# Squares of the channel products from an SBUF copy, and another bank for each later batch's last state outputs

## The chip, the core and the metric

One core of a Trainium2 chip runs the whole program. The metric is device microseconds (us) of one execution; smaller is better. The core has a matrix engine (PE, whose weight loads are listed as PEld), a vector engine (DVE), a scalar engine (ACT), a small general engine (POOL), and DMA queues, which are issued here from SP. Matrix products land in PSUM, of which this kernel uses eight banks; ACT and DVE read them out to SBUF.

## What is computed

Four batches of 768 time steps with 384 channels go through three layers, one after the other:

```python
# 1. a complex linear recurrence per head (8 heads of 48), real part kept
S_re, S_im = ar * S_re - ai * S_im + k v^T,  ar * S_im + ai * S_re
y[t] = q[t] @ S_re
# 2. two pairs of products with a Relu between them
u = x + (relu(x^T @ w_tok1) @ w_tok2)^T
z = u + relu(u @ w_ch1) @ w_ch2
# 3. mixing with the step before, and a squared Relu
xk = mu_k * z + (1 - mu_k) * z_prev ;  xr = mu_r * z + (1 - mu_r) * z_prev
out = sigmoid(xr @ w_r) * (relu(xk @ w_k) ** 2 @ w_v)
```

`w_k` is 384 x 1024 and `w_v` 1024 x 384. Everything is float32 outside; inside, a number is split in two float16 parts (high and low) and a product of two such numbers takes three matrix products: high by high, high by low, low by high.

## The kernel before, in words

**Two streams.** A generator `attention(b)` makes layer 1 of batch b, in six blocks J of 128 time steps; a generator `dense(b)` makes layers 2 and 3. While `dense(b)` is issued, pieces of `attention(b + 1)` are issued between its pieces by a schedule of due times. The order of the instructions on each engine is then fixed at compile time by a planner, which has priorities (the `tc.high_priority` blocks: evacuations 400, the recurrence's matrix products 100) and its own estimate of each duration. On the chip every engine runs its list in that order, and waits at the head of it.

**Layer 3's first product.** `two_layers` runs through 16 items a batch (two halves t of the time steps, eight column blocks f). For an item, `wk1` issues nine matrix products into a PSUM tile `ps` of 128 x 384; `wk1_out` (lines 907 to 911) turns it into the two float16 parts of the square, `part[:, 0]` and `part[:, 1]`; `wv2` multiplies these with `w_v` in nine more products, which come in the program two items later (`LAG`). `ps` comes from a pool of two banks (`ps_d`), which the gate (`wr`) and the earlier layers use too. `wk1_out` squares in place: ACT does Relu (L908) and Square (L909) from `ps` to `ps`, ACT copies it to `part[:, 0]` (L910), and DVE subtracts that from `ps` to make `part[:, 1]` (L911). The bank is held until L911 has ended.

**Layer 1's outputs.** Each block J has a state product (`s_u`, bank tag `u`) and its outputs (`s_h`, bank tag `y`, in two groups g of four heads). Either tag has one bank in batches 2 to 4. For a head, `s_h` issues three products with the carried state `T16` (seen in the trace as `y<-CH,Rc 96*128`) and three with the masked scores `M16` (`y<-CH,Rc 128*128`). `M16` comes from the scores `sp` by DVE (`m<-sp,tri`), then ACT (`Rc<-m`), then DVE (`Rc<-m,Rc`). `s_i` reads the outputs out: ACT `xh<-y`, then DVE `xl<-y`, after which the bank is free for the next block. `s_u` of the last block, J = 5, issues nothing. The recurrence's products all have line L482 in the trace, and its ACT and DVE work line L337.

At the start of the next batch's layer 1, `X` (the decay inputs) is loaded by DMA, squared on ACT (`X<-X`, `wide<-X`) and added on DVE (`X<-X,wide`).

The SBUF tiles with tags `h1h` and `h1l` hold layer 2's first result (`h1`, 128 x 2 x 384 float16 each); they lie idle once `w_tok2` has been applied.

Of the kernel before, what the change touches and what calls it, by code (L numbers as in the profile page):

```python
# [8 lines left out]
F32 = mybir.dt.float32  # L9
# [4 lines left out]
ACTF = mybir.ActivationFunctionType  # L14
# [3 lines left out]
B, H, S, D = 4, 8, 768, 48  # L18
C = H * D
NJ = S // 128  # L20
# [35 lines left out]
X_S, U_S, XK_S, XR_S, SQ_S = 6, 5, 5, 3, 14  # L56
T1_S, T2_S, C1_S, C2_S, WK_S, WV_S, WR_S = 6, 5, 6, 7, 6, 6, 3
# [43 lines left out]
def split_path(  # L101
# [10 lines left out]
    MUL, ADD, SUB, MAX, MIN = ALU.mult, ALU.add, ALU.subtract, ALU.max, ALU.min  # L112
# [9 lines left out]
    TT = nc.vector.tensor_tensor  # L122
# [3 lines left out]
    ACT = nc.scalar.activation  # L126

    const = ctx.enter_context(tc.tile_pool(name="const", bufs=1))
    one = ctx.enter_context(tc.tile_pool(name="one", bufs=1))
# [56 lines left out]
    def seen(x):  # L186

        j = one.tile([128, LOW_N], F16, tag="seen", name="seen")
        if len(x.shape) == 3:
            j = j.rearrange("p (a f) -> p a f", a=x.shape[1])  # L190
        ACT(j, x, ACTF.Square, accum_out=col("low"))
# [126 lines left out]
    def hd(x):  # L318
        return x.rearrange("p (h d) -> p h d", h=H)
# [5 lines left out]
    last_ev = []  # L325
    tables = [None, [], []]

    def attention(b):
# [3 lines left out]
        st, hl, at = {}, {}, [None]  # L332

        def chained(fn, last):

            def call(*a, **k):
                ins = fn(*a, **k)  # L337
                if b == 0 and at[0] is not None:
                    last[:] = behind([ins], last)
                return ins  # L340

            return call

        on_act, on_dve = [], []
        ACT = chained(nc.scalar.activation, on_act)
        TT, STT = (chained(f, on_dve) for f in (nc.vector.tensor_tensor, nc.vector.scalar_tensor_tensor))
# [57 lines left out]
        def bank(tag, J, shape):  # L404
            if b == 0 and J % 2:
                return ps_a.tile(shape, F32, tag={"u": "a0", "y": "a1"}[tag], name=tag)
            return ps_1.tile(shape, F32, tag=tag, name=tag)
# [73 lines left out]
        def MM(**k):  # L481
            last_mm[:] = [nc.tensor.matmul(**k)]  # L482
            behind(last_mm, ahead if b == 0 else passed)
# [184 lines left out]
        def s_h(J, g):  # L668
            d = st[J]
            if g == 0:  # L670
                d["y"] = bank("y", J, [128, H, D])
            y = d["y"]
            with tc.high_priority(offset=P_PE):
                for h in range(4 * g, 4 * g + 4):
                    if J > 0:
                        th, tl = hd(T16[0:96, J % 2]), hd(T16[0:96, 2 + J % 2])
                        for n_, (a_, b_) in enumerate((("h", th), ("h", tl), ("l", th))):
                            MM(out=y[:, h], lhsT=Tr[J % 2]["q" + a_][0:96, h], rhs=b_[:, h], start=n_ == 0, stop=False)
                    if b == 0:
                        MM(out=y[:, h], lhsT=d["m", g][:, h % 4], rhs=d["v32"][:, h], start=J == 0, stop=True)  # L680
                    for n_, (m_, v_) in enumerate(((0, "vh"), (0, "vl"), (1, "vh")) if b > 0 else ()):
                        MM(out=y[:, h], lhsT=M16[g][m_][:, h % 4], rhs=d[v_][:, h], start=J == 0 and n_ == 0, stop=n_ == 2)
            return 0.0
# [24 lines left out]
        cq, ck = late(s_c, "q"), late(s_c, "k")  # L708
        fns = {"a": s_a, "x": s_x, "l": s_l, "b": s_b, "w": s_w, "q": cq, "k": ck, "e": s_e, "i": s_i, "u": s_u, "v": s_v}
        fns.update({nm + str(g): late(fn, g) for nm, fn in (("f", s_f), ("g", s_g), ("h", s_h), ("m", s_m)) for g in range(2)})  # L710
        order = [(x[0], fns[x[:-1]], int(x[-1])) for x in (ORD0 if b == 0 else ORD1).split()]

# [38 lines left out]
    def dense(b):  # L751
# [9 lines left out]
        h1 = [one.tile([128, 2, C], F16, tag=f"h1{s}", name=f"h1{s}") for s in "hl"]  # L761
        for f in range(2):
            need(("t1", f))
            if b == 0:
                ps = h1_ps[f][:, 0:N]
            else:
                ps = ps_d.tile([128, N], F32, tag="d", name="ps")
# [11 lines left out]
        u = [[two.tile([128, 3, N], F16, tag=f"u{s}", name=f"u{s}") for s in "hl"] for t in range(2)]  # L779
        for t in range(2):  # L780
            need(("t2", t))
            for c in range(3):
                ps = ps_d.tile([128, N], F32, tag="d", name="ps")
# [12 lines left out]
        def two_layers(nf, first, second, evac1, evac2, at=None):  # L796

            items = [(t, f) for t in range(2) for f in range(nf)]
            parts, acc = {}, {}
            for n_ in range(len(items) + LAG):  # L800
                if n_ < len(items):
                    t, f = items[n_]
                    ps = ps_d.tile([128, N], F32, tag="d", name="ps")
                    first(t, f, ps)
                    part = gring.tile([128, 2, N], F16, tag="g", name="g")
                    with tc.high_priority(offset=P_EV):
                        evac1(ps, part)
                        if n_ == 0:
                            seen(part[:, 0, 0:LOW_N])
                    parts[t, f] = part  # L810
                    yield 9 * MM
                    if at and n_ in at:
                        yield from at[n_]()
                if n_ >= LAG:
                    t, f = items[n_ - LAG]
                    if f == 0:
                        acc[t] = [ps_a.tile([128, N], F32, tag=f"a{i}", name=f"a{i}") for i in range(3)]
                    part = parts.pop((t, f))
                    for i in range(3):
                        second(t, f, i, part, acc[t][i], f == 0, f == nf - 1)  # L820
                        if f == nf - 1:
                            evac2(t, i, acc[t][i])
                    yield 9 * MM
# [8 lines left out]
            for c in range(3):  # L832
                mm3(ps, [w[:, c, 128 * f:128 * f + 128] for w in wc1], [x[:, c] for x in u[t]], c == 0, c == 2)

        def ch1_out(ps, part):
            ACT(part[:, 0], ps, ACTF.Relu)  # L836
            last_ev[:] = [STT(part[:, 1], ps, 0.0, part[:, 0], op0=MAX, op1=SUB)]  # L837

# [58 lines left out]

        NF = FC // 128
        yield from two_layers(NF, ch1, ch2, ch1_out, ch2_out, {NF + 10: lambda: gate(0)})


# [2 lines left out]
            for c in range(3):  # L904
                mm3(ps, [w[:, c, 128 * f:128 * f + 128] for w in wk], [x[:, c] for x in xk[t]], c == 0, c == 2)

        def wk1_out(ps, part):
            ACT(ps, ps, ACTF.Relu)  # L908
            ACT(ps, ps, ACTF.Square, scale=2.0 ** (SQ_S // 2 - XK_S - WK_S))  # L909
            ACT(part[:, 0], ps, ACTF.Copy)  # L910
            last_ev[:] = [TT(part[:, 1], ps, part[:, 0], op=SUB)]  # L911

        def wv2(t, f, jj, part, ps, start, stop):
            need(("v", f))
# [2 lines left out]
        def wv2_out(t, jj, ps):  # L917
# [4 lines left out]
            nc.sync.dma_start(out=out[b, 128 * J:128 * J + 128, :], in_=o)  # L922

        yield from two_layers(FK // 128, wk1, wv2, wk1_out, wv2_out, {FK // 128 + LAG: lambda: gate(1)})

    def run(gen, got, want):
# [319 lines left out]
```

## Time and profile before

| | us |
|---|---|
| median of 3 runs | 816.45 (816.13 to 817.19) |
| the profiled execution | 818.82 |
| its span, first to last instruction | 817.0 |
| PE busy in it | 741.3 (91%) |
| DVE busy | 581.8 (71%) |
| ACT busy | 522.6 (64%) |
| mean granted TensorE clock | 0.974 of full speed |

The profiled execution is 1.8 us longer than its span, and 2.4 us longer than the median. Busy time is what an engine spent in instructions; matrix products are pipelined, so that a row of 128 x 384 products shows 326 to 331 ns each while one starts every 0.16 us. Idle time of an engine is put down to the instruction that it waited for.

### The profile page before, as it was taken

The page shows a single profiled execution, that of the slowest core. Times are in us where ns is not written, and L with a number is a line of the kernel's source. Part 1 is how long each engine was busy: PE and PEld are TensorE (multiplying, and loading weights), DVE is VectorE, ACT ScalarE, POOL GpSimd, SP SyncE. Part 2 cuts the span into 40 slices and gives each one's busy share as a digit, 9 for nine tenths or more (in the row PEclk, how much of TensorE's full clock was granted, in tenths as well). Part 3 has the DMA queues.
Part 4 walks back from the last instruction along what each step waited for, and adds up shares of the span by engine and source line. Part 5 has one row for each costly group of instructions (what it writes and reads, how often), then busy time and mean ns, then how long its engine had stood idle before and what let it go on. Part 6 is the DMA issues. An engine that isn't in the chain of part 4 may idle for free.

```text
span 817.0 us, 15178 instructions
## 1 busy us (share of the span) xinstructions
PE 741.3 (91%) x6107; PEld 471.4 (58%) x6107; DVE 581.8 (71%) x1016; ACT 522.6 (64%) x988; POOL 21.3 (3%) x53
## 2 busy tenths in 40 slices
PE   0968878999989889999998989999999999999996
PEld 0557845455555455555665656566666666666553
DVE  3998978999998738887768448777776454484822
ACT  7884559777588779674568778566576532142752
POOL 3000000001010000000000000000000000010000
PEclk9987989999999999999999989999999999999998
DMA  8249983444673851052336331141333342868200
GB/s 273 78 118 205 195 264 136 130 154 118 176 137 82 194 120 49 20 122 55 62 63 120 91 85 49 46 104 26 63 62 63 81 134 79 268 198 261 103 30 33
DMA packets 137949, 94.92 MB, mean 116 GB/s; under 512 B 104592, under 2 KB 120208, under 8 KB 137872
## 3 DMA queue, kind: packets, MB, share of 16 engines
q1 hardware_dynamic: 137872, 93.88, 45.2%
q8 instruction: 50, 0.82, 0.4%
q14 instruction: 27, 0.22, 0.1%
HBM read 63.97 MB, written 4.72 MB: 84 GB/s over the span
## 4 chain that ended last, share of the span: by engine, by line
PE 47%; DVE 21%; ACT 15%; DMA 12%; issue 3%; SPq 1%; DVEq 0%; ACTq 0%
PE ps L741 22%; PE a L741 14%; PE y L482 4%; DVE X L337 4%; ACT X L337 3%; DMA X<-by_time_a_re_dram 3%; PE u L482 3%; DMA wst<-in_moe_w_k_dram 2%; DVE Wc L337 2%; PE sp L482 2%; ACT tmp L875 2%; DMA Rc<-qh 1%; DVE g L837 1%; DMA wst<-in_moe_w_v_dram 1%; DVE ql L337 1%
## 5 line engine op out<-in xcount | busy, mean ns | idle before, releaser
L741 PEld LDWEIGHTS <-wc 128*128 128x128 f16 x1728 | 166.7, 98 | 116.9 <-issue 9.5
L741 PE MATMUL ps<-uh,wc 128*128 128x384 f16 x576 | 156.3, 326 | 2.1 <-DVE ul L793 1.2
L741 PE MATMUL a<-g,wc 128*128 128x384 f16 x864 | 157.9, 326 | 0.0
L741 PE MATMUL ps<-xkh,wk 128*128 128x384 f16 x384 | 106.4, 331 | 3.5 <-DVE g L911 3.3
L741 PE MATMUL a<-wv,g 128*128 128x384 f16 x576 | 106.9, 328 | 2.5 <-ACT g L910 2.5
L836 ACT ACTIVATE g<-ps 128x384 f16<-128x384 f32 x96 | 46.4, 484 | 78.0 <-PE ps L741 76.6
L741 PE MATMUL ps<-ul,wc 128*128 128x384 f16 x288 | 93.8, 326 | 0.0
L482 PEld LDWEIGHTS <-Rc 96*128 96x128 f16 (+1 forms) x1416 | 69.8, 100 | 34.4 <-issue 13.9
L837 DVE SCALAR_TENSOR_TENSOR g<-ps,g 128x384 f16<-128x384 f32 x96 | 52.9, 554 | 37.4 <-ACT g L836 37.2
L741 PEld LDWEIGHTS <-wk 128*128 128x128 f16 x576 | 55.6, 99 | 39.9 <-issue 6.4
L741 PEld LDWEIGHTS <-g 128*128 128x128 f16 x576 | 54.9, 98 | 37.4 <-ACT g L910 3.0
L741 PE MATMUL ps<-xkl,wk 128*128 128x384 f16 x192 | 63.5, 331 | 0.0
L911 DVE TENSOR_TENSOR g<-ps,g 128x384 f16<-128x384 f32 x64 | 35.3, 553 | 35.1 <-ACT g L910 34.9
L482 PE MATMUL y<-CH,Rc 96*128 96x48 f16 (+1 forms) x912 | 42.9, 186 | 9.7 <-DVE xl L337 5.2
L908 ACT ACTIVATE ps<-ps 128x384 f32<-128x384 f32 x64 | 30.4, 476 | 30.9 <-PE ps L741 29.5
L337 DVE TENSOR_TENSOR m<-sp,tri 128x512 f32<-128x512 f32 x48 | 32.6, 685 | 20.5 <-PE sp L482 19.7
L482 PE MATMUL sp<-Rc 96*128 96x128 f16 x504 | 39.2, 225 | 8.6 <-DVE m L337 3.3
L337 DVE TENSOR_TENSOR Wc<-cs,X 128x768 f32<-128x768 f32 x48 | 44.8, 951 | 0.2
L337 ACT ACTIVATE X<-X 128x1152 f32<-128x1152 f32 x32 | 37.1, 1159 | 11.5 <-DMA X<-by_time_a_re_dram 9.6
L337 ACT ACTIVATE X<-X,col_c 128x1152 f32<-128x1152 f32 x32 | 40.0, 1252 | 1.2 <-DVE X L337 0.4
L482 PE MATMUL u<-CH,kh 128*128 128x48 f16 x320 | 36.2, 188 | 3.4 <-ACT kh L337 3.4
L337 DVE TENSOR_TENSOR Rc<-m,Rc 128x512 f16<-128x512 f32 x36 | 24.8, 689 | 18.6 <-ACT Rc L337 18.6
(212 smaller groups left out, 1377.9 us busy)
## 6 DMA issues: line engine op xcount, KB each, us to landing
wst<-in_moe_w_ch_dram SPq DMA_DIRECT2D x24, 768.0 KB, 4.4
CH<-in_qk_dram SPq DMA_DIRECT2D x18, 384.0 KB, 3.2
wst<-in_moe_w_tok_dram SPq DMA_DIRECT2D x8, 768.0 KB, 5.0
wst<-in_moe_w_k_dram SPq DMA_DIRECT2D x8, 768.0 KB, 4.5
wst<-in_moe_w_v_dram SPq DMA_DIRECT2D x8, 768.0 KB, 4.6
X<-by_time_a_re_dram SPq DMA_DIRECT2D x8, 576.0 KB, 4.8
X<-by_time_a_im_dram SPq DMA_DIRECT2D x8, 576.0 KB, 6.9
CH<-by_time_v_dram SPq DMA_DIRECT2D x24, 192.0 KB, 2.7
```

The lines of the kernel that those rows point to most:

```text
L337: ins = fn(*a, **k)
L482: last_mm[:] = [nc.tensor.matmul(**k)]
L741: ins = [nc.tensor.matmul(out=ps, lhsT=lh[a_], rhs=rh[b_], start=start and n_ == 0, stop=stop and n_ == 2) for n_, (a_, b_) in enumerate(( ...
L836: ACT(part[:, 0], ps, ACTF.Relu)
L837: last_ev[:] = [STT(part[:, 1], ps, 0.0, part[:, 0], op0=MAX, op1=SUB)]
L875: ACT(w[:, 0:N], z[:, 0:N], ACTF.Copy, scale=o[:, c:c + 1])
L908: ACT(ps, ps, ACTF.Relu)
L911: last_ev[:] = [TT(part[:, 1], ps, part[:, 0], op=SUB)]
```

## The change

Two edits. In `wk1_out` the Relu now goes from PSUM to a float32 SBUF tile `r` (in the idle `h1h` and `h1l` places, by the parity of f), with the scale that the Square had. In batch 1 (b == 0) ACT squares `r` in place and copies it to `part[:, 0]`, as before but from SBUF. In batches 2 to 4 ACT squares `r` straight into `part[:, 0]`, and DVE makes the float32 square by multiplying `r` with itself in place. DVE's subtraction then reads `r`. So `ps` has one reader, the Relu. In `s_h` the outputs of the last block of batches 2 to 4 use the bank tagged `u` in place of `y`. The argument f is passed on to both evacuation functions.

```diff
         def s_h(J, g):
             d = st[J]
             if g == 0:
-                d["y"] = bank("y", J, [128, H, D])
+                d["y"] = bank("u" if b > 0 and J == NJ - 1 else "y", J, [128, H, D])
...
-                        evac1(ps, part)
+                        evac1(ps, part, f)
...
-        def ch1_out(ps, part):
+        def ch1_out(ps, part, f):
...
-        def wk1_out(ps, part):
-            ACT(ps, ps, ACTF.Relu)
-            ACT(ps, ps, ACTF.Square, scale=2.0 ** (SQ_S // 2 - XK_S - WK_S))
-            ACT(part[:, 0], ps, ACTF.Copy)
-            last_ev[:] = [TT(part[:, 1], ps, part[:, 0], op=SUB)]
+        def wk1_out(ps, part, f):
+            r = one.tile([128, C], F32, tag=f"h1{'hl'[f % 2]}", name="r")
+            ACT(r, ps, ACTF.Relu, scale=2.0 ** (SQ_S // 2 - XK_S - WK_S))
+            if b == 0:
+                ACT(r, r, ACTF.Square)
+                ACT(part[:, 0], r, ACTF.Copy)
+            else:
+                ACT(part[:, 0], r, ACTF.Square)
+                TT(r, r, r, op=MUL)
+            last_ev[:] = [TT(part[:, 1], r, part[:, 0], op=SUB)]
```

## Rows read from the trace of the kernel before

**Rows 1.** The page's busy us, share of the span and instructions of each engine.

```profile
PE 741.3 (91%) x6107; PEld 471.4 (58%) x6107; DVE 581.8 (71%) x1016; ACT 522.6 (64%) x988; POOL 21.3 (3%) x53
```

**Rows 2.** Waits of PE: who waited for whom; us in total, times, longest.

```profile
PE y L482 <- DVE xl L337: 5.2, 2, 2.8
...
PE ps L741 <- DVE g L911: 3.3, 4, 2.6
...
PE a L741 <- ACT g L910: 2.5, 2, 1.3
```

**Rows 3.** Groups by line: xcount | busy us, mean ns | idle before, releaser.

```profile
L911 DVE TENSOR_TENSOR g<-ps,g 128x384 f16<-128x384 f32 x64 | 35.3, 553 | 35.1 <-ACT g L910 34.9
...
L910 ACT ACTIVATE g<-ps 128x384 f16<-128x384 f32 x64 | 30.9, 483 | 0.9
L908 ACT ACTIVATE ps<-ps 128x384 f32<-128x384 f32 x64 | 30.4, 476 | 30.9 <-PE ps L741 29.5 <-DVE g L911 1.4
```

**Rows 4.** Groups by line, the forms nearest to what is added.

```profile
L337 ACT ACTIVATE X<-u 128x384 f32<-128x384 f32 x24 | 11.7, 487 | 3.5 <-PE u L439 1.6 <-PE u L482 1.6
...
L877 ACT ACTIVATE xkh<-tmp 128x384 f16<-128x384 f32 x24 | 12.4, 516 | 2.5 <-DVE tmp L876 2.5
...
L864 DVE TENSOR_TENSOR tmp<-tmp,ul 128x384 f32<-128x384 f32 x18 | 8.9, 552 | 0.0
```

**Rows 5.** The chain that ended last, 784 to 806 us: start, us, what.

```profile
797.02 1.46 PE ps L741 x9
```

**Rows 6.** Timeline, 440 to 450 us: start, us, engine, line, operation.

```profile
442.31 0.47 ACT L908 ACTIVATE ps<-ps 128x384 f32<-128x384 f32 x1
...
445.49 0.47 ACT L909 ACTIVATE ps<-ps 128x384 f32<-128x384 f32 x1
445.62 1.36 DVE L337 TENSOR_TENSOR X<-X,wide 128x1152 f32<-128x1152 f32 x1 [2.04 <-ACT wide L337]
...
447.35 0.56 DVE L911 TENSOR_TENSOR g<-ps,g 128x384 f16<-128x384 f32 x1 [0.37 <-ACT g L910]
...
447.96 0.32 PE L741 MATMUL ps<-xkh,wk 128*128 128x384 f16 x1 [2.56 <-DVE g L911]
```

**Rows 7.** Timeline, 474 to 495 us.

```profile
481.21 0.47 ACT L908 ACTIVATE ps<-ps 128x384 f32<-128x384 f32 x1
...
483.90 0.62 ACT L337 ACTIVATE Rc<-m 128x512 f16<-128x512 f32 x1
...
485.06 0.68 DVE L337 TENSOR_TENSOR Rc<-m,Rc 128x512 f16<-128x512 f32 x1
485.19 0.20 PE L482 MATMUL y<-CH,Rc 96*128 96x48 f16 x1 [2.77 <-DVE xl L337]
```

**Rows 8.** Timeline, 296 to 312 us.

```profile
296.98 0.47 ACT L908 ACTIVATE ps<-ps 128x384 f32<-128x384 f32 x1 [0.86 <-PE ps L741]
...
302.73 0.55 DVE L911 TENSOR_TENSOR g<-ps,g 128x384 f16<-128x384 f32 x1
...
306.54 0.61 ACT L337 ACTIVATE Rc<-m 128x512 f16<-128x512 f32 x1
...
306.93 0.28 PE L482 MATMUL y<-CH,Rc 96*128 96x48 f16 x3 [2.39 <-DVE xl L337]
```

**Rows 9.** Stretches: us, busy us of PE, PEld, DVE, ACT, POOL, granted clock, DMA.

```profile
421.00:450.00 29.00, 25.64 (x242) 16.39 (x241) 24.27 (x47) 23.35 (x46) 0.00 (x0) 1.00 0.53 106
600.00:630.00 30.00, 28.15 (x269) 18.01 (x268) 23.04 (x47) 24.43 (x54) 0.00 (x0) 1.00 0.40 67
307.00:311.00 4.00, 4.00 (x43) 2.68 (x43) 3.82 (x6) 2.74 (x6) 0.00 (x0) 0.58 0.00 0
...
484.00:492.00 8.00, 6.81 (x55) 4.47 (x55) 4.81 (x8) 6.87 (x12) 0.00 (x0) 0.57 0.01 2
```

**Rows 10.** Groups by line on DVE, 421 to 450 us; then 600 to 630 us.

```profile
L911 DVE TENSOR_TENSOR g<-ps,g 128x384 f16<-128x384 f32 x6 | 3.3, 552 | 0.4 <-ACT g L910 0.4
...
L911 DVE TENSOR_TENSOR g<-ps,g 128x384 f16<-128x384 f32 x9 | 4.9, 552 | 0.4 <-ACT g L910 0.4
```

## The prediction, made before the changed kernel ran

> **What bounds the kernel now.** I read four views: the page's busy shares, the waits of PE, the timeline around the longest of those waits, and stretches for clock and load. PE is busy for 91% of the span, DVE for 71% and ACT for 64% [rows 1]. Towards the end, with no recurrence left, PE runs nine products in 1.46 us, back to back, and nothing else matters [rows 5]. So PE's own work is the floor, and the change adds and removes no matrix product. What can change is the time in which PE stands still. Three waits of PE lead to what is edited: outputs waiting for `xl` to leave the bank `y` (5.2 us, two times), first products waiting for L911 to free a `ps` bank (3.3 us, four times), and second products waiting for L910 (2.5 us, two times) [rows 2]. Together they are 11.0 us. [...]
>
> **The `ps` bank.** Before, an item's bank is held through Relu, Square, Copy and the subtraction; after, through the Relu alone. The largest case stands at 448 us: the Relu ended at 442.78, but L909 was at 445.49 and L911 at 447.35, and PE stood still for 2.56 us until it had ended [rows 6]. With the change the bank is free at 442.8, before PE begins to wait, so this wait goes. Next late is the second product of the same item. Its high part is the new Square, in L909's place, done at about 446.0. Its low part needs two DVE operations of 0.55 us, which queue behind `X<-X,wide`, which ends at 446.98 [rows 6]: about 448.1, where it was 447.9. The second products come in the list after nine first ones (1.46 us [rows 5]), so 445.4 + 1.46 = 446.9 is the soonest that they are wanted, and up to 1.2 us can come back for those that read the low part. I let half of it come back, so 2.0 us for this wait, and count all of the other three (3.3 - 2.56 = 0.74): 2.7 us. Bounds: 0 (the list places other waiting work there) and 3.3.
>
> **The bank of the last outputs.** `T16` is made from the same bank `u`, so outputs that read `T16` never find `u` occupied: this adds no wait. It removes the wait for `xl`, but not for `M16`, which the other half of the outputs reads. At 485 us PE resumed at 485.19; ACT's `Rc<-m` ended at 484.52 and DVE's `Rc<-m,Rc` at 485.74 [rows 7]. At 307 us PE resumed at 306.93, and `Rc<-m` ended at 307.15 [rows 8]. So alone this edit moves only the `T16` products forward, about 0.3 us for each of two ends; I take 0.6 us. Together with the bank edit more follows. At 303 us the bank freed by L911 at 303.28 would be free from the Relu that ended at 297.45 [rows 8], and at 485 us the Relu at 481.21 frees one at 481.68, inside the 2.77 us in which PE stood still [rows 7]. Nine first products (1.46 us [rows 5]) then fit into either wait, 2.9 us. Sum 3.5 us; bounds 0 and 5.2 [rows 2].
>
> **The head of each layer 3.** In batches 2 to 4 the high part is made by two ACT operations instead of three, so about 0.48 us [rows 3] less for each of the two waits for L910: 1.0 us. Bounds 0 and 2.5 [rows 2].
>
> **The clock.** The two stretches lose 0.42 x 4 = 1.7 and 0.43 x 8 = 3.4 us [rows 9], 5.1 us in all. They begin with waits of 2.4 and 2.8 us; the wait of 2.56 us at 448 us lies in a stretch at 1.00 [rows 6, 9], so length alone does not decide. With shorter waits the lower level may stay away or not. I take a third, 1.7 us; bounds 0 and 5.1.
>
> **What ACT and DVE pay.** Nothing in the trace is a Square from SBUF of this size; the nearest rows are 516 ns for an ACT operation from SBUF to float16 and 487 ns from PSUM to float32 SBUF [rows 4]. Before, three ACT operations take 476 + 476 + 483 = 1435 ns [rows 3]. Batch 1: 487 + 516 + 516 = 1519, 84 ns more for each of 16 items, 1.3 us on ACT, hidden behind PE where ACT is not what PE waits for. I take 0.5; bounds 0 and 1.3. Batches 2 to 4: 487 + 516 = 1003 ns, 0.43 us less for each of 48 items, 20.7 us of ACT, which is no bottleneck; I count no more for it than is counted above. DVE gets 48 multiplications; the nearest row, two float32 operands from SBUF, takes 552 ns [rows 4], 26.5 us in all. The subtraction now reads SBUF, 552 against 553 ns [rows 3, 4]: no change. The cover is DVE's idle time. It is thin at two heads of layer 3: DVE is busy for 24.27 of 29 us and 23.04 of 30 us [rows 9], with six and nine items [rows 10]. They become 24.27 + 6 x 0.55 = 27.6 (95%) and 23.04 + 9 x 0.55 = 28.0 (93%). Queued behind each multiplication are `m`, `Rc`, `xl` and the shifted inputs of the next half, and PE waits for those. I take 1.5 us; bounds 0 (the work all falls into the 4.7 and 7.0 us of idle time) and 15 x 0.55 = 8.3 (each delays PE in full).
>
> [...]
>
> **Sum.** 2.7 + 3.5 + 1.0 + 1.7 = 8.9 us gained; 0.5 + 1.5 = 2.0 us paid: -6.9 us. The profiled execution took 818.82 us, so 811.9 for one like it. It lies 2.4 us above the median of the runs, 816.45; the same step from the median gives 809.6 us, which I predict.
>
> **Rivals.** *The gaps stay, only what is waited for changes.* An engine's order is fixed, so an early bank is used only if the next instruction of PE's list needs it. For this rival: both long waits end when ACT and DVE catch up, and `M16` comes 0.2 to 0.5 us after the bank [rows 7, 8]; `m`, `Rc` and the second products all hang on the same DVE queue. Against: the 2.56 us at 448 are a wait for nothing but the bank [rows 6]. What is left is 0.7 for the short waits and 0.6 for the `T16` products, less 0.5: 0.8 us, so 815.6 us, within the 0.2% (1.6 us) that a measurement of this kernel can tell from no change.
>
> *DVE becomes the bound at the heads of batches 2 and 3* (the slower side). The place is the first 25 to 30 us of layer 3, the price up to 8.3 us. In this case the waits for banks turn into waits for the low part, so that only 0.7 (short waits), 0.6 (`T16`) and 1.0 (heads) stay gained, less 0.5 on ACT: 1.8 us. It decides once more than three of the 15 multiplications delay PE in full (4 x 0.55 = 2.2). Half of them: 8.3 / 2 - 1.8 = 2.3 us more, 818.8; all 15: 8.3 - 1.8 = 6.5 us more, 823.0. For it: 95% and 93%, and a low part whose chain now crosses from ACT to DVE once and then needs two operations there. Against: the evacuations have the highest priority of the planner, which knows the added work, and 4.7 us were idle.
>
> [...]
>
> **How the numbers follow.** Forecast 0.50, full clock 0.15, gaps stay 0.15, DVE the bound 0.20. The forecast's own range, from its bounds, is 805 to 814. The range that should hold 8 in 10 reaches down to the full clock's 803 and up to 818.5, into the half-delayed case of DVE; left out is most of the DVE rival and little below. Faster by over 0.2%: 0.50 + 0.15 and a third of the gaps case, 0.70. Within 0.2%: the rest of that and a little of DVE's, 0.13. Slower: 0.17.
>
> **What would show it.** The page's wait "first products for DVE L911" must be gone, and none for a Relu in its place of more than a few tenths. PE's wait for `xl` must be gone, replaced by one for `Rc` of under 1.5 us. The granted clock after 307 and 485 us (a few us earlier in the new trace) shows the clock's term. ACT's busy time should fall by about 19 us and DVE's rise by about 26; DVE in the first 30 us of layer 3 of batches 2 and 3 must have idle time left. The prediction is wrong if PE's waits for the subtraction, `m` or `Rc` grow there by more than 5 us, or if the planner sets PE's list so that the freed bank is not used.

## The result, and the profile after

The changed kernel took 809.9 us (median of four runs, 805.76 to 811.41) beside 816.82 us for the kernel before on the same chip: a ratio of 0.9894, 95% interval 0.9866 to 0.9922. In a later set it was 0.9902 (0.9882 to 0.9923). So it is faster by about 1%: 8 to 9 us by the ratios, 6.9 us between the two medians, where 6.9 were forecast; the forecast time of 809.6 rests on a median 0.4 us lower. The profiled execution took 809.93 us, its span 808.1.

The page's busy row, and some rows of the waits of PE:

```profile
PE 741.2 (92%) x6107; PEld 472.2 (58%) x6107; DVE 603.7 (75%) x1064; ACT 506.2 (63%) x940; POOL 21.2 (3%) x53
```

```profile
PE u L482 <- ACT Rc L337: 3.6, 2, 2.4
PE sp L482 <- DVE m L337: 3.5, 5, 1.5
...
PE y L482 <- DVE Rc L337: 2.2, 4, 0.8
...
PE u L482 <- DVE Rc L337: 1.2, 1, 1.2
...
PE a L741 <- DVE g L916: 0.8, 3, 0.4
```

Two of the three waits of [rows 2] are gone: nobody waits for `xl` to leave a bank, and no first product waits for the subtraction (now L916) or for the Relu that frees its bank now (L909). The third, for the high part, became 0.8 us for the low part. But in the place of the wait for `xl`, products of the recurrence now wait 3.6 us for ACT's `Rc`, a row that was not among the long ones before.

The groups of the evacuation answer to [rows 3, 4]:

```profile
L916 DVE TENSOR_TENSOR g<-r,g 128x384 f16<-128x384 f32 x64 | 35.5, 554 | 4.6 <-ACT g L912 3.2
...
L909 ACT ACTIVATE r<-ps 128x384 f32<-128x384 f32 x64 | 30.9, 482 | 33.5 <-PE ps L741 33.4
...
L915 DVE TENSOR_TENSOR r<-r 128x384 f32<-128x384 f32 x48 | 26.6, 553 | 24.3 <-ACT g L914 24.1
L914 ACT ACTIVATE g<-r 128x384 f16<-128x384 f32 x48 | 25.0, 521 | 1.1
```

DVE had the added 26.6 us of L915 and yet its busy time rose only from 581.8 to 603.7, by 21.9; ACT's fell by 16.4 us. Records of instructions that stand back to back overlap here (L915 at 446.06 us takes 0.56, and the next on DVE begins at 446.54, 0.08 before that ends; 48 x 0.08 is 3.8 us, as an estimate), so that busy time moved by less than the durations, and by less than the 26 and 19 us of the forecast.

**A stretch that starts at one instruction.** The spans contain a start-up that varies: the first product of layer 3 of batch 1 began between 227.3 and 232.5 us in the profiles of this study, where its work is the same. So I compare from that product to the end of the span. Columns as in [rows 9]; first the kernel before (all of it, then layer 3 of batch 2), then the kernel after:

```profile
232.44:817.00 584.56, 552.39 (x4557) 347.91 (x4554) 380.61 (x700) 358.48 (x711) 10.51 (x31) 0.98 0.38 96
...
422.06:496.02 73.96, 67.78 (x660) 44.43 (x658) 46.32 (x82) 59.08 (x103) 0.00 (x0) 0.95 0.40 88
```

```profile
231.93:808.10 576.17, 548.67 (x4557) 345.01 (x4554) 402.73 (x748) 342.00 (x663) 10.48 (x31) 0.99 0.39 97
...
420.27:488.93 68.66, 64.97 (x658) 42.33 (x656) 53.21 (x98) 53.53 (x87) 0.00 (x0) 1.00 0.42 94
```

The stretch is 8.4 us shorter, with the same 4557 products. PE's busy time fell by 552.39 - 548.67 = 3.7 us, and the rest, in which PE stood still, from 32.2 to 27.5, by 4.7. As an estimate from the granted clock, most of the 3.7 is the clock's (3.4, worked out in the part on the prediction). Layer 3 of batch 2 alone gives 5.3 us of the 8.4 (2.8 busy, 2.5 still), and its mean clock went from 0.95 to 1.00.

**Three places.** First the wait at 448 us of [rows 6]. The timeline of after, around the same products:

```profile
439.08 0.48 ACT L909 ACTIVATE r<-ps 128x384 f32<-128x384 f32 x1
...
443.53 0.33 PE L741 MATMUL ps<-xkh,wk 128*128 128x384 f16 x1
...
446.19 0.34 PE L741 MATMUL a<-wv,g 128*128 128x384 f16 x1 [0.25 <-DVE g L916]
```

The Relu, ended at 439.56, frees the bank 4.0 us before the first product at 443.53, and of the 2.56 us a wait of 0.25 for the low part is left.

Second, the end of batch 3's recurrence ([rows 7], then 485 us):

```profile
479.44 0.20 PE L482 MATMUL u<-CH,Rc 128*128 128x48 f16 x1 [1.17 <-ACT Rc L337]
...
481.49 0.65 PE L482 MATMUL u<-CH,Rc 128*128 128x48 f16 x19 [1.22 <-DVE Rc L337]
```

One wait of 2.77 became two of 1.17 and 1.22, for `Rc`.

Third, the end of batch 2's recurrence ([rows 8], then 307 us). Here nothing was won. First the kernel before, then after:

```profile
301.46 1.17 ACT L337 ACTIVATE X<-X 128x1152 f32<-128x1152 f32 x1 [2.98 <-DMA X<-by_time_a_re_dram]
301.46 1.35 DVE L384 TENSOR_REDUCE stat_rmin<-X 128x1 f32<-128x1152 f32 x1 [4.62 <-DMA X<-by_time_a_re_dram]
...
303.93 0.61 PE L482 MATMUL sp<-Rc 96*128 96x128 f16 x8 [1.31 <-DVE m L337]
```

```profile
298.68 1.17 ACT L337 ACTIVATE X<-X 128x1152 f32<-128x1152 f32 x1 [3.07 <-DMA X<-by_time_a_re_dram]
298.68 1.35 DVE L384 TENSOR_REDUCE stat_rmin<-X 128x1 f32<-128x1152 f32 x1 [4.81 <-DMA X<-by_time_a_re_dram]
...
300.12 1.28 ACT L337 ACT_TABLE_LOAD   x1 [0.27 <-DVE stat_rmin L384]
300.42 0.68 DVE L337 TENSOR_TENSOR m<-sp,tri 128x512 f32<-128x512 f32 x1
301.16 0.22 PE L482 MATMUL sp<-Rc 96*128 96x128 f16 x1 [1.51 <-DVE m L337]
...
303.73 0.63 ACT L337 ACTIVATE Rc<-m 128x512 f16<-128x512 f32 x1
...
304.41 0.26 PE L482 MATMUL u<-CH,Rc 128*128 128x48 f16 x2 [2.40 <-ACT Rc L337]
```

Read it from the top: ACT and DVE both stand at the decay inputs of the next batch, which have not landed (3.07 and 4.81 us; 2.98 and 4.62 before). `m` waits in DVE's queue behind them: after's products for it had ended by 297.91 us, and it began at 300.42, behind the minimum that stood at the load (298.68) and L916 (299.95). `Rc` waits in ACT's, behind the same load and then a table load (`ACT_TABLE_LOAD`, 1.28 us), more work on `X` and three shorter operations: `m` had ended at 301.10, and `Rc` began at 303.73. PE's list has recurrence products next. A free `ps` bank is of no use there: the next first product, at 304.57, stands in the list behind the ones that wait.

The stretches at the heads of batches 2 and 3, and at the ends of the recurrences:

```profile
419.00:448.00 29.00, 27.85 (x268) 17.90 (x267) 27.25 (x55) 22.04 (x43) 0.00 (x0) 1.00 0.54 107
593.00:623.00 30.00, 29.00 (x274) 18.50 (x272) 27.20 (x57) 21.14 (x45) 0.00 (x0) 1.00 0.41 67
302.00:310.00 8.00, 5.60 (x44) 3.29 (x44) 4.86 (x7) 6.47 (x12) 0.00 (x0) 0.57 0.03 6
...
476.00:484.00 8.00, 5.61 (x65) 3.69 (x63) 5.13 (x9) 7.97 (x12) 0.00 (x0) 1.00 0.01 2
```

DVE is at 27.25 of 29 and 27.20 of 30 us, with idle time left, as worked out (27.6 and 28.0). The clock was 1.00 in the 8 us from 476 and 0.57 in the 8 us from 302. In the other profiled execution of the same kernel (after, again) it was 0.79 over the same 8 us:

```profile
302.00:310.00 8.00, 6.30 (x68) 4.04 (x69) 5.18 (x8) 7.10 (x13) 0.00 (x0) 0.79 0.10 25
```

A third change lies in a place that the prediction did not look at. Before, PE waited 2.30 us in batch 1, and the clock behind it was 0.66 over 5 us; after, the wait is 0.48 and the clock 1.00. The wait and the stretch before, then both after:

```profile
278.90 0.65 PE L482 MATMUL y<-CH,Rc 128*128 128x48 f16 x19 [2.30 <-DVE Rc L337]
...
279.00:284.00 5.00, 5.00 (x38) 2.75 (x38) 4.64 (x6) 3.48 (x5) 0.00 (x0) 0.66 0.61 161
```

```profile
277.27 0.65 PE L482 MATMUL y<-CH,Rc 128*128 128x48 f16 x19 [0.48 <-DVE Rc L337]
...
279.00:284.00 5.00, 4.57 (x50) 2.86 (x48) 3.06 (x5) 4.71 (x9) 0.00 (x0) 1.00 0.11 40
```

### The profile page after: what moved, and what is told of

It reads as the page before. It is cut to its first block, busy times and chain, and to the rows that moved or that the text cites. A ratio compares the mean times of both kernels' runs of the same rounds, so it can differ in the third digit from the quotient of the medians.

```text
span 808.1 us, 15175 instructions
## 1 busy us (share of the span) xinstructions
PE 741.2 (92%) x6107; PEld 472.2 (58%) x6107; DVE 603.7 (75%) x1064; ACT 506.2 (63%) x940; POOL 21.2 (3%) x53
## 4 chain that ended last, share of the span: by engine, by line
PE 49%; DVE 24%; ACT 12%; DMA 11%; issue 3%; SPq 0%; DVEq 0%; ACTq 0%
PE ps L741 22%; PE a L741 16%; DVE X L337 4%; PE y L482 4%; ACT X L337 4%; PE u L482 3%; DVE Wc L337 2%; DMA X<-by_time_a_re_dram 2%; DMA wst<-in_moe_w_k_dram 2%; PE sp L482 2%; DVE tmp L876 2%; DVE g L837 1%; DMA wst<-in_moe_w_v_dram 1%; ACT L337 1%; DVE tmp L858 1%
## 5 line engine op out<-in xcount | busy, mean ns | idle before, releaser
L482 PEld LDWEIGHTS <-Rc 96*128 96x128 f16 (+1 forms) x1416 | 68.7, 100 | 36.0 <-issue 9.2
L909 ACT ACTIVATE r<-ps 128x384 f32<-128x384 f32 x64 | 30.9, 482 | 33.5 <-PE ps L741 33.4
L482 PE MATMUL sp<-Rc 96*128 96x128 f16 x504 | 38.3, 223 | 9.0 <-DVE m L337 3.5
L337 DVE TENSOR_TENSOR Wc<-cs,X 128x768 f32<-128x768 f32 x48 | 44.9, 953 | 0.1
L915 DVE TENSOR_TENSOR r<-r 128x384 f32<-128x384 f32 x48 | 26.6, 553 | 24.3 <-ACT g L914 24.1
L337 DVE TENSOR_TENSOR m<-sp,tri 128x512 f32<-128x512 f32 x48 | 32.6, 686 | 14.7 <-PE sp L482 14.5
L337 ACT ACTIVATE X<-X 128x1152 f32<-128x1152 f32 x32 | 37.0, 1160 | 10.3 <-DMA X<-by_time_a_re_dram 8.8
L337 ACT ACTIVATE X<-X,col_c 128x1152 f32<-128x1152 f32 x32 | 39.9, 1253 | 1.1 <-DVE Rc L337 0.4
L482 PE MATMUL u<-CH,kh 128*128 128x48 f16 x320 | 36.5, 188 | 3.5 <-ACT kh L337 3.4
L482 PE MATMUL y<-CH,Rc 96*128 96x48 f16 (+1 forms) x768 | 35.4, 184 | 4.1 <-DVE Rc L337 2.2
L916 DVE TENSOR_TENSOR g<-r,g 128x384 f16<-128x384 f32 x64 | 35.5, 554 | 4.6 <-ACT g L912 3.2
```

The costliest lines, as they stand in the source:

```text
L909: ACT(r, ps, ACTF.Relu, scale=2.0 ** (SQ_S // 2 - XK_S - WK_S))
L915: TT(r, r, r, op=MUL)
L916: last_ev[:] = [TT(part[:, 1], r, part[:, 0], op=SUB)]
```

## The experiments

Each kernel was timed in five rounds beside the kernel before; ratios are to that one, with 95% intervals. The last column is the stretch from layer 3's first product to the end in the profile (before 584.56, after 576.17). The first four kernels ran on one chip, the next four on a second and the last three on a third.

| kernel | median us | ratio | stretch us |
|---|---|---|---|
| only the outputs' bank | 816.93 | 0.9992 (0.9969 to 1.0014) | 586.56 |
| without the outputs' bank | 810.22 | 0.9913 (0.9885 to 0.9940) | 577.98 |
| after, `ps` held as long as before | 815.95 | 0.9978 (0.9951 to 1.0006) | 584.54 |
| three ACT operations in all batches | 809.49 | 0.9917 (0.9892 to 0.9943) | 578.71 |
| DVE multiplies in all batches | 804.54 | 0.9824 (0.9794 to 0.9853) | 572.29 |
| one more DVE operation, first halves | 813.94 | 0.9946 (0.9918 to 0.9973) | 581.33 |
| one more DVE operation, second halves | 810.25 | 0.9877 (0.9851 to 0.9903) | 576.90 |
| decay inputs behind the read-out | 804.61 | 0.9820 (0.9795 to 0.9844) | 571.74 |
| both that and DVE in all batches | 805.20 | 0.9849 (0.9826 to 0.9872) | 571.70 |
| the same, both halves behind | 807.78 | 0.9880 (0.9855 to 0.9904) | 575.06 |
| after, again | 809.43 | 0.9902 (0.9882 to 0.9923) | 575.81 |

Two limits hold for all that follows. An interval is about 2 us to either side, and that of a difference between two rows about 3; a stretch is that of one execution (after's two gave 576.17 and 575.81). And each kernel is planned anew, so that the lists of the engines differ in places from after's; no run holds the order fixed.

My theory was that the early release of `ps` carries most of the gain. The rivals were the outputs' bank, and ACT's shorter chain.

**Only the outputs' bank**: the kernel before with the edit in `s_h` alone.

```diff
-                d["y"] = bank("y", J, [128, H, D])
+                d["y"] = bank("u" if b > 0 and J == NJ - 1 else "y", J, [128, H, D])
```

> Only the outputs' bank is changed; the squares are made in PSUM as before. Bank theory (the gain of 7 us is the early release of the first products' bank): the outputs still wait for M16, so about 0.6 us less than before, 816.2 (815.3 to 816.8). Rival (the waits for xl and the low clock behind them, 5.2 + 5.1 us, are what the change removed): 807 to 811.

No change within the interval, which reaches from 2.5 us faster to 1.1 slower. Its middle, 0.7 us, is near the 0.6 of the prediction, but does not confirm it: the profile's stretch is 2.0 us longer than before's. Its waits of PE:

```profile
PE u L482 <- ACT Rc L337: 4.1, 2, 2.5
PE ps L741 <- DVE g L911: 3.9, 4, 3.1
```

The wait for `xl` has gone and one for `Rc` has come; the `ps` wait stays, its longest 3.1 us where it was 2.6.

**Without the outputs' bank**: the kernel after with that line put back.

> Only the squares are changed; the last outputs keep bank y. Bank theory: nearly the whole gain, 810 to 811.5, with no wait for L911 left in the trace and the wait for xl back at 485 us. Rival (outputs' bank): 813 to 816.5.

```profile
PE y L482 <- DVE xl L337: 4.9, 2, 2.6
```

The wait for `xl` is back with 4.9 us, and the time does not tell from that of after (0.9913 beside 0.9894 and 0.9902). So the other edit brings the gain. A wait of 5 us at the top of the list was worth 0.9 to 1.6 us by the middles of the ratios and about 2 by the stretch, which is not told from nothing: what follows it was late anyway.

**`ps` held as long as before**: a small copy reads the bank when the subtraction has been made, so that it comes free then; all else as in after.

```diff
             last_ev[:] = [TT(part[:, 1], r, part[:, 0], op=SUB)]
+            hold = one.tile([128, 1], F32, tag="cnt", name="hold")
+            behind([nc.vector.tensor_copy(hold, ps[:, 0:1])], last_ev)
```

> The changed kernel, with one DVE copy of a single column of ps added behind each subtraction, so that the bank is held as long as before although ACT has its two operations. It adds 64 DVE instructions of about 0.1 us. Bank theory: the waits for the bank come back, 2.7 + 2.9 us and part of the clock: 814.5 to 818. Rival (the 20 us that ACT is relieved of make the gain): within 1.5 us of the changed kernel, 810 to 811.5.

Most of the gain is gone: 0.9978. Its waits of PE, the longest of them for `m`, the copy's group, and the stretch:

```profile
PE sp L482 <- DVE m L337: 6.7, 6, 2.5
...
PE ps L741 <- DVE hold L918: 2.1, 4, 0.8
PE a L741 <- ACT g L914: 1.9, 2, 1.4
```

```profile
449.17 0.83 PE L482 MATMUL sp<-Rc 96*128 96x128 f16 x12 [2.48 <-DVE m L337]
```

```profile
L918 DVE COPY hold<-ps 128x1 f32<-128x1 f32 x64 | 9.6, 151 | 0.0
```

```profile
231.16:815.70 584.54, 552.25 (x4557) 345.99 (x4554) 407.85 (x812) 341.62 (x663) 10.51 (x31) 0.99 0.38 96
```

The copies themselves, 0.151 us each where about 0.1 was expected, cost something too. By the next experiment but one, DVE time in the first halves of batches 2 and 3 costs under half of itself: 16 copies there, some 1.1 us as an estimate; batch 1's eight at most 1.2. Of the (0.9978 - 0.9902) x 818 = 6.2 us that were lost, some 3.9 are thus the bank's by the middles of the intervals; no run has the copies without the hold. Busy time too is back at 552.25, 3.6 above after's. The granted clock shows a part of that: 0.98 from 419 to 495 us here and 1.00 from 420 to 489 in after, 0.02 x 76 = 1.5 us as an estimate. The wait for the bank itself came back only in part, 2.1 us with a longest of 0.8: at the place of the 2.56 us, PE now stands 2.48 us for `m`, because its list has products of the recurrence there.

**Three ACT operations in all batches**: ACT squares and copies as in batch 1, and DVE multiplies nowhere.

```diff
-            if b == 0:
-                ACT(r, r, ACTF.Square)
-                ACT(part[:, 0], r, ACTF.Copy)
-            else:
-                ACT(part[:, 0], r, ACTF.Square)
-                TT(r, r, r, op=MUL)
+            ACT(r, r, ACTF.Square)
+            ACT(part[:, 0], r, ACTF.Copy)
```

> The changed kernel with batch 1's form in all batches: three ACT operations, Square and Copy from SBUF, no multiplication on DVE. The bank is freed early, ACT is not relieved (0.08 us more than before for each item). Bank theory: 809 to 811.5, heads 1 us worse, DVE 1.5 us better. Rival (ACT's relief): 814 to 817.

Equal within the interval. So the gain needs neither ACT's relief nor DVE's multiplication: with the Relu moved out of PSUM, three ACT operations bring most of it too. Whether relief and load in batches 2 to 4 are both small or cancel (the prediction had 1.0 gained at the heads and 1.5 paid) is not told apart; the profile alone shows this kernel 2.5 us longer than after.

**One more DVE operation**, `TT(r, r, r, op=MAX)`, which changes no value, on the 16 items of the first halves of batches 2 and 3 (the heads), and in another kernel on the 16 of the second halves.

```diff
...
                 TT(r, r, r, op=MUL)
+                if b < 3 and t == 0:
+                    TT(r, r, r, op=MAX)
```

> The changed kernel with one more DVE operation of the same size (the larger of r and r, which changes nothing) for each of the 16 items in the first halves of layer 3 of batches 2 and 3, 8.8 us of DVE in the crowded stretches. Prediction's term (1.5 of 8.3 us reach PE): 811 to 813. Rival (DVE is the bound there already): 815 to 819. Free: 809 to 810.5.

> The same additional operation in the second halves (16 items, 8.8 us) of batches 2 and 3, where DVE is busy for half of the time. Both theories of the DVE term: no change, 809 to 811. If it is the longer chain of each item and not DVE's load that costs, as much as in the first halves.

In the heads 8.8 us of DVE cost (0.9946 - 0.9902) x 818 = 3.6 us, or 4.3 by after's first ratio; in the second halves nothing. Nearly all of the cost lies in batch 2: from its first product of layer 3 to batch 3's it took 177.9 us beside after's 173.7, and from there to batch 4's 154.5 beside 154.1, although DVE was fuller in batch 3. The windows of the heads in the first of the two:

```profile
418.00:447.00 29.00, 26.69 (x253) 16.68 (x252) 26.69 (x57) 19.35 (x37) 0.00 (x0) 1.00 0.42 92
596.00:626.00 30.00, 28.79 (x269) 18.20 (x266) 29.96 (x63) 21.32 (x45) 0.00 (x0) 1.00 0.34 67
```

Even with DVE at 29.96 of 30 us PE does 28.79 us of work: a full DVE did not by itself stop PE there. Why batch 2 pays and batch 3 does not was not tested.

**DVE multiplies in all batches**: batch 1 too takes two ACT operations and the multiplication.

```diff
-            if b == 0:
-                ACT(r, r, ACTF.Square)
-                ACT(part[:, 0], r, ACTF.Copy)
-            else:
-                ACT(part[:, 0], r, ACTF.Square)
-                TT(r, r, r, op=MUL)
+            ACT(part[:, 0], r, ACTF.Square)
+            TT(r, r, r, op=MUL)
```

> The changed kernel with the multiplication on DVE in batch 1 too (16 more, 8.8 us of DVE; ACT 16 operations fewer). DVE was busy for 28.5 of the first 30 us of batch 1's layer 3 before the change. If DVE work delays PE where DVE is full (the prediction's DVE term): 2 to 6 us slower than the changed kernel, 812 to 816. If DVE work is free even there: 809 to 811. If ACT is what matters in batch 1: 806 to 809.

It is faster than after by some 5 us (6.4 by the ratios, 3.9 by the stretches). The head of batch 1's layer 3:

```profile
227.00:257.00 30.00, 27.68 (x251) 16.82 (x250) 30.00 (x60) 24.11 (x52) 2.48 (x4) 1.00 0.44 84
```

In after, the first 30 us there show DVE at 29.19 and ACT at 27.49. So DVE was made full and ACT shorter by 3.4 us, and the time fell: DVE's load is not what PE hangs on in batch 1. The waits at 301 and 304 us of after are 0.80 and 1.65 us here, though ACT stands at the same load:

```profile
292.81 1.16 ACT L337 ACTIVATE X<-X 128x1152 f32<-128x1152 f32 x1 [3.39 <-DMA X<-by_time_a_re_dram]
...
296.25 0.62 ACT L337 ACTIVATE Rc<-m 128x512 f16<-128x512 f32 x1
...
298.98 1.28 ACT L337 ACT_TABLE_LOAD   x1
```

`Rc` stands ahead of the table load here, and behind it in after (303.73 and 300.12). This points to ACT's list; whether its length counts or its order, no run tells.

**Decay inputs behind the read-out.** This goes at the third place above: the squares and the minimum of the second half of the decay inputs of batches 3 and 4 are ordered behind the read-out (`xh`, `xl`) of the previous batch's last outputs, so that ACT and DVE don't stand at a DMA before `m` and `Rc`.

```diff
...
-            if b == 1:
+            if b == 1 or (b > 1 and k == 1):
                 behind([ins], last_copy)
...
-                RED(col("rmin"), X1[:, i], axis=AX.XY, op=MIN)
+                ins = RED(col("rmin"), X1[:, i], axis=AX.XY, op=MIN)
+                if b > 1 and k == 1:
+                    behind([ins], last_low)
...
-            if b == 0 and J == NJ - 1:
-                last_copy.append(ins)
-            STT(xl[:, J], yv, col_c[:, 3:4], xh[:, J], op0=MUL, op1=SUB)
+            if J == NJ - 1:
+                last_copy[:] = [ins]
+            ins = STT(xl[:, J], yv, col_c[:, 3:4], xh[:, J], op0=MUL, op1=SUB)
+            if J == NJ - 1:
+                last_low[:] = [ins]
```

> The changed kernel with ACT's squares and DVE's minimum of the second half of the next batch's decay inputs (batches 3 and 4) ordered behind the read-out of the last outputs of the batch before, so that ACT and DVE don't stand at the head of their lists waiting for that load while the last outputs need them. If the waits that are left at 301 to 304 and 479 to 482 us come from there: these 6 us of waits and the low clock behind them go, 803 to 807. If the next batch's recurrence then comes too late: 811 to 818. If neither: 809 to 811.

0.9820. Timeline at the end of batch 2's recurrence, and the stretch of 8 us there (L338 and L485 are after's L337 and L482, L914 its L909):

```profile
298.98 0.63 ACT L338 ACTIVATE Rc<-m 128x512 f16<-128x512 f32 x1 [1.74 <-DVE m L338]
...
299.97 0.49 ACT L914 ACTIVATE r<-ps 128x384 f32<-128x384 f32 x1 [0.35 <-PE ps L746]
...
300.40 0.65 PE L485 MATMUL u<-CH,Rc 128*128 128x48 f16 x19 [0.18 <-DVE Rc L338]
```

```profile
300.00:308.00 8.00, 7.82 (x67) 4.80 (x64) 5.47 (x11) 7.86 (x10) 0.00 (x0) 1.00 0.14 50
...
229.36:801.10 571.74, 547.10 (x4556) 344.30 (x4554) 403.33 (x748) 341.58 (x663) 10.49 (x31) 0.99 0.39 98
```

The waits of 1.51 and 2.40 us are a few tenths, ACT no longer stands at a DMA, the clock is 1.00 there, and the stretch is 4.4 us shorter than after's. So the cause of the third place is not a bank, but what stood at the front of two queues: a load, and the work on `X` behind it, which moved back with it and was not told apart from it. All of the gain lies there: from batch 1's first product of layer 3 to batch 2's it took 183.3 us beside after's 188.3, and from batch 2's to batch 3's 173.7 in both kernels. At the end of batch 3's recurrence the same edit saved nothing.

**Both**, and then with the squares and the minimum of the first half ordered behind too.

> The multiplication on DVE in all batches (as in e5_mul_all) and the later squares of e7_squares together. If the two act on different waits (ACT's list in all of batch 1's layer 3; the load at the ends of the recurrences): their gains add up to 9 or 10 us below the changed kernel, 799 to 801.5. If both remove the same wait at 301 to 304 us: 803 to 805.

> As e9_both, with the squares of the first half ordered behind the last outputs too. If ACT's standing wait for the first half's load costs PE time as the second's did: 1 to 3 us less than e9_both. If the next batch's recurrence then starts too late for the layers that follow: 3 us more or worse.

The two do not add up: 0.9849 beside 0.9824 and 0.9820, and stretches of 571.70, 572.29 and 571.74. Both shorten the same part: from batch 1's first product of layer 3 to batch 2's it is 188.3 us in after, 183.4 with DVE in all batches, 183.3 with the decay inputs moved and 182.9 with both. Then something else sets the time. Ordering the first half behind as well brings nothing more (183.5 us) and may give some back (0.9880).

**After, again**, beside these:

> The changed kernel itself, on the chip of the two above, for an interval of its own: ratio to the kernel before 0.986 to 0.993.

0.9902, in the middle of that range, with a stretch of 575.81 us beside 576.17.

## Why the prediction was right

The direction, the time and the cause that was ranked first held; the sum's terms were less good than the sum, and the close agreement of the time is in part luck.

- **The `ps` bank**, 2.7 us: right in kind. The waits for L911 (3.3 us) are gone and 0.25 of the longest is left; I had let up to half of 1.2 us come back. With the bank held, some 3.9 us of about 8 are lost by the middles of the intervals, more than 2.7; some 1.5 us of what was lost went with the clock, as an estimate.
- **The outputs' bank alone**, 0.6 us: 0.7 by the middle of an interval of some 2 us to either side, which does not test it. The wait for `xl` did turn into waits for `Rc`, but the longest is 2.4 us, not under 1.5.
- **First products that fit into the two long waits**, 2.9 us: wrong. At 485 us, 0.4 came back (2.77 to 1.17 + 1.22). At 307 us nothing did (1.31 for `m` and 2.39 before, 1.51 and 2.40 after). The prediction's own condition, that the freed bank is used only where PE's list has a first product next, was not met; and I took `M16` as late by itself, where it was late behind a DMA that ACT and DVE stood at, as the trace of the kernel before already shows (2.98 and 4.62 us at 301.46).
- **The heads**, 1.0 us: the waits for L910, 2.5 us, became 0.8 for the low part: 1.7.
- **The clock**, 1.7 us: too small in all. Of the two low stretches of [rows 9], the later went (3.4 us) and the earlier grew, from 0.42 x 4 = 1.7 us lost to 0.43 x 8 = 3.4; together that is the 1.7 of the forecast, but by a gain and a loss that it did not foresee. A third low stretch, at 279 us before, was not in the sum; it went too, for another 0.34 x 5 = 1.7. The 3.4 us are most of the 3.7 by which the busy time of equal products fell. These figures are estimates from the mean granted clock of one execution each. The changed kernel does not show the clock back in full, from which the range has its lower end of 803: in the 8 us from 302 it was 0.57 and 0.79.
- **ACT and DVE**, 2.0 us paid: not borne out as a share of DVE's time. I had taken 1.5 / 8.3 = 0.18 of the added time; one more operation in the same places costs 3.6 to 4.3 of 8.8, 0.41 to 0.48, but nearly all of it in batch 2. What the multiplications of the change themselves cost is not known: the kernel without them in any batch is no faster. ACT's 1.3 us in batch 1 were taken as nearly hidden; the kernel with DVE in all batches points to ACT's list there, its length or its order, for some 5 us.

In sum, idle time of PE gave 4.7 us where 8.9 - 1.7 - 2.0 = 5.2 were forecast, and PE's busy time 3.7 where 1.7 were forecast from the clock: two errors of opposite sign. The time came within 0.3 us of the forecast, but the ratio makes the gain 8.7 us and the stretches make it 8.4. Of the 2.9 us for first products 2.5 did not come; the clock, partly in a place that was not in the sum, made up for them. The rival in which the gaps stay was right about the waits at both ends (0.4 of 2.77 us came back at one, nothing at the other), but not about the clock at the later one. DVE as the bound did not come, though it was near: 8.8 us more in the heads takes back half of the gain.

The prices of the operations came close to the rows that they were taken from: the Square from SBUF took 521 ns (516 taken), the Relu out of PSUM 482 (487), the multiplication 553 (552), and the subtraction 554 from SBUF, where it was 553 from PSUM.

Open: why DVE in all batches brings as much as moving the decay inputs; both shorten the same waits and both have ACT's `Rc` ahead of the table load there, but the lists of all engines differ in order, and no run isolates it. How much of the main gain is the bank's release itself, and how much the other order that the planner can set with it, is open for the same reason. Nor is it known what sets the time once both further edits are made.

## What to carry to other kernels

A bank that one instruction reads comes free before one that a chain works on in place (at 448 us before, the Relu had ended at 442.78 and the subtraction at 447.91); what that is worth is not the wait for it but what PE's list has next, so follow the wait one step further: here 5 us of waiting for one bank were worth some 1 to 2, not told from nothing, and 3.3 for the other some 4. Where PE waits for an instruction of ACT or DVE, look at what stands ahead of it in that queue: at one of two such places, a DMA that ACT and DVE both wait for, with the work behind it, cost as much as half of the whole change gave (4.4 of 8.4 us by the stretches), and ordering three instructions behind the read-out took it away; at the other the same edit gave nothing. Compare from a fixed instruction to the end, with busy and idle time apart, when the start-up of a kernel varies by more than the effect.

## What the runs showed of the hardware

The clock did not follow the length of a single wait. Before, waits of 2.30 us that end at 278.90 and of 2.77 at 485.19 came with a clock of 0.50 in the stretches of 280 to 283 and 485 to 491 us, and one of 2.56 that ends at 447.96 with 1.00 from 448 to 449; after, 1.51 and 2.40 us that end at 301.16 and 304.41 came with a mean of 0.57 over 8 us, and 1.17 and 1.22 that end at 479.44 and 481.49 with 1.00. The same kernel at the same place gave 0.57 in one execution and 0.79 in another. A DVE copy of one element per partition out of PSUM took 151 ns.
